# Batch 0's last pairs in another order, and w_in's loads cut at an eighth

## The chip, the core and the metric

The kernel runs on one core of a Trainium2 chip. The metric is the device time of one execution in microseconds (us). The core has five engines that run side by side and meet at semaphores: TensorE (PE, matmuls; its weight loads are shown apart as PEld), VectorE (DVE), ScalarE (ACT), GpSimd (POOL) and SyncE (SP). DMAs are issued by POOL's queue and by SP's queue and are carried by 16 shared DMA engines. A DMA that POOL issues also takes POOL some time to describe.

## The reference

Attention with a window of 32 tokens and 8 global tokens, for 8 batches, 8 heads, 576 tokens and 64 values a head; its output, 4608 tokens of 512, goes through two matrices with a snake function between them:

```python
scores = scale * np.matmul(q, k.transpose(0, 1, 3, 2))
mask = np.abs(pos[:, None] - pos[None, :]) <= window
mask = mask | is_global[:, None] | is_global[None, :]
scores = np.where(mask, scores, -1000000000.0)
...
attn = attn / (np.sum(attn, axis=-1, keepdims=True) + 1e-09)
x = np.matmul(attn, v)                    # then heads side by side: (4608, 512)
h = x @ w_in                              # (512, 2048)
s = np.sin(alpha * h)
g = h + s * s / (alpha + 1e-09)
out = g @ w_out                           # (2048, 512)
```

## The kernel before

**Stages.** The batches run one after the other: the attention of batch b+1 shares PE with gemm2 of batch b, and gemm1 of batch b+1 follows. The order of instructions on each engine is written out by hand; each engine takes its own in that order. Batch 0 has no gemm2 to run beside it: until about 28 us there is attention alone (`first_batch`), then gemm1(0), and at 51 us the attention of batch 1 with gemm2(0) begins.

**Attention.** Heads go in four pairs (`hp` 0 to 3, `last` is 3). For each pair `scores` makes products of queries and keys in PSUM, two parts with an Exp on ACT that writes the weights E, and `cover` multiplies E by the mask on DVE. `denominators(hp)` sums the weights with matmuls by ones into zd, then ACT takes a logarithm L (L772), SP stores it, and DVE sums eight columns for the global tokens (GD, L756). `inverse(hp)` is one Exp on ACT from L to R (L779; two buffers). `first_numerators(hp)` does `products(hp, 0)` (28 matmuls), `global_products` (8 matmuls) and `normalise`, which on DVE multiplies by R into xT (L908) and sums GN. In batch 0 the numerators of pairs 0 and 2 lie in the bank zr, those of pair 1 in zn, and those of pair 3, like all denominators, in zd. So each use of zd waits until L and GD have read the one before it.

**`set_recip`** turns alpha on PE (L710), copies it to alphaT (L711), adds 1e-9 (L712) and takes the reciprocal into recipT (L713), all on DVE behind the transpose. alphaT is the scale of gemm1's Sin (L1162); recipT enters gemm1's last step, H on DVE (L1168). `warm(z, n)` issues n spare matmuls of 128x512 into a bank that nobody reads (L569).

**gemm1** makes 16 groups of 128 columns (`nt`), each of 4 chunks (one for each pair of heads) in two halves. Groups 0 and 1 first do the chunks of pairs 0 to 2, six matmuls each, and then that of pair 3, which needs the last xT. Then come Sin on ACT, the square on ACT or DVE, and H on DVE.

**gemm2** multiplies H by w_out in blocks of 128 rows. gemm2(0) does, for its first two blocks, matmuls 0 to 7 of both ahead; then block 0 goes on with matmul 8. `fill(n)` issues the next n of them: 7 before the attention of batch 1 begins and 9 within its first pair, then 9 within the second.

**Loads.** POOL issues, in this order: lying copies of batch 0's q and k (`load_lying`), v (`load_v0`, 12 DMAs), the first part of w_in, then, after `pace` has waited for the last pair's weights E, the second part of w_in, batch 1's q and k for pairs 0 and 1, the third part of w_in, q and k for pairs 2 and 3, v of batch 1 (`cast_v(1)`, tile vd), and w_out in two halves (`load_w_out`, matmuls 0 to 7 and 8 to 15). They leave in order from one queue. Meanwhile SP's queue gathers the rows of the global tokens from v, k and q. `load_w_in(lo, hi)` counts in quarters of the 2048 columns, so its first part, `load_w_in(0, 1)`, covers groups 0 to 3, the second groups 4 to 7, the third 8 to 15.

Of the kernel before, what the change touches and what calls it, by code (L numbers as in the profile page):

```python
# [249 lines left out]
def kernel(  # L250
# [13 lines left out]
    DM, DFF = moe_w_in.shape  # L264
# [83 lines left out]
    def cast_v(b):  # L348
        cast_heads(b, v, "vd")

    def pace(src):

        nc.gpsimd.tensor_copy(out=seen[0 : src.shape[0]], in_=src)
# [43 lines left out]
    def edge_tile(half):  # L397
        r, o = half * D, (1 - half) * D
        m = (1 - half) * NT6
        nc.vector.tensor_copy(out=VX[0][r : r + KT, m], in_=VX[0][o : o + KT, 1 if m else NT6 - 1])  # L400
# [21 lines left out]

    def load_w_in(lo, hi):
        if lo < hi:
            cols = slice(lo * DFF // 4, hi * DFF // 4)
            nc.gpsimd.dma_start(
                out=w_in[:, :, cols], in_=moe_w_in[:, cols].rearrange("(c p) n -> p c n", p=P)
            )
# [24 lines left out]
    def load_lying(b, w, hps):  # L453

        hs = slice(2 * hps.start, 2 * hps.stop)
        nc.gpsimd.dma_start(
            out=lie[b][D * w : D * w + NU, hs],
            in_=(q, k)[w][b, hs].rearrange("h (u r) d -> u h (r d)", r=NR),
        )
# [3 lines left out]
    zo = [banks.tile([P, 512], DT.float32, name=f"zo{i}") for i in range(2)]  # L463
# [103 lines left out]
    def warm(z, n):  # L567
        for _ in range(n):
            nc.tensor.matmul(  # L569
                out=z[:], lhsT=ones[:], rhs=ones[:][:, None, :].to_broadcast([P, 4, P]),  # L570
                start=True, stop=True, skip_group_check=True,
            )
# [133 lines left out]
        nc.tensor.matmul(out=zo[0][:], lhsT=pick[:], rhs=VGb[:], start=True, stop=True, skip_group_check=True)  # L706
        nc.vector.tensor_copy(out=VGT[:].rearrange("p h d -> p (h d)"), in_=zo[0][:])

    def set_recip():
        nc.tensor.transpose(out=zo[0][:, 0:NT], in_=arow[:], identity=idf[0:NT, 0:NT])  # L710
        nc.vector.tensor_copy(out=alphaT[:], in_=zo[0][:, 0:NT])  # L711
        nc.vector.tensor_scalar(out=recipT[:], in0=alphaT[:], scalar1=1e-9, scalar2=None, op0=ALU.add)  # L712
        nc.vector.reciprocal(out=recipT[:], in_=recipT[:])  # L713

# [39 lines left out]
    def global_sums(b, hp, key, z):  # L754
        g0 = z[:, 0, 0, 0:4]
        nc.vector.tensor_reduce(  # L756
            out=(GN, GD)[key][:, hp, :, b].rearrange("p (c x) -> p x c", x=2),
            in_=bass.AP(
                tensor=g0.tensor, offset=g0.offset,
                ap=[list(g0.ap[0]), [256, 2], [1, 4], [512, 2], [SEG, 4]],  # L760
            ),
            axis=AX.XY, op=ALU.add,
        )

    def tokens(z):
        return z.rearrange("p k x c -> p (k x) c")[:, :, 0 : 3 * SEG].rearrange(
            "p k (m c) -> p k m c", c=SEG
        )[:, :, :, 4:]
# [8 lines left out]
    def inverted(L):  # L777
        R = normp.tile([P, 4, 3, KT], DT.float32, name="R")
        nc.scalar.activation(out=R[:], in_=L[:], func=AF.Exp, scale=-1.0, bias=shift[:, 0:1])  # L779
        return R  # L780

    def attention(b, beside):
# [43 lines left out]
        def weights(hp, g):  # L826
            return Es[hp][:, :, G3 * g : G3 * (g + 1), :].rearrange("p t m c -> p t (m c)")

        def cover(hp, g):
            Eg = weights(hp, g)  # L830
            nc.vector.tensor_tensor(  # L831
                out=Eg, in0=Eg,
                in1=MASKT[:, None, G3 * g : G3 * (g + 1), :].rearrange("p o m c -> p o (m c)").to_broadcast(
                    [P, 2, G3 * WCOL]
                ),
                op=ALU.mult,
            )

        def nd(hp, key):


            if b == 0:
                t = zd if key or hp == last else (pair["zr"], zn)[hp % 2]
            else:
                t = (zn, zd)[key] if hp < last else (pair["zr"] if key else zd)
            return t[:].rearrange("p k (x c) -> p k x c", x=2)

        def products(hp, key):


            for e in range(NT6 + 1):
                for half in range(2):
                    i, m, c0, c1 = windows(half)[e]
                    s0 = begin(i)
                    lo, hi = (0, CUT + 4) if half == 0 else (CUT, QLEN)
                    if e == NT6:
                        lo, hi = (lo, CUT) if half == 0 else (CUT + 4, hi)
                    a, z = max(s0 + c0, lo), min(s0 + c1, hi)
                    rows = slice(half * D, half * D + NK)
                    for t in range(2):  # L860
                        bank = (hp, key, half, t)
                        nc.tensor.matmul(  # L862
                            out=nd(hp, key)[t * D : (t + 1) * D, half, :, a - half * CUT : z - half * CUT],
                            lhsT=ones[rows, 0:D] if key else values(b, rows, half, i, 2 * hp + t),
                            rhs=Es[hp][rows, t, m, :].rearrange("p (x c) -> p x c", x=2)[:, :, a - s0 : z - s0],
                            start=bank not in begun, stop=True, skip_group_check=True,
                        )
                        begun.add(bank)

        def global_products(hp):  # L870


            for half in range(2):
                rows = slice(half * D, half * D + NK)
                for t in range(2):
                    for x in range(2):
                        e0 = Es[hp][rows, t, 0, 60 * x + 20 : 60 * x + 21]
                        nc.tensor.matmul(
                            out=nd(hp, 0)[t * D : (t + 1) * D, half, x, 0 : 3 * SEG].rearrange(
                                "p (m c) -> p m c", c=SEG  # L880
                            )[:, :, 4:],
                            lhsT=VGT[rows, 2 * hp + t, :],
                            rhs=bass.AP(
                                tensor=e0.tensor, offset=e0.offset,
                                ap=[list(e0.ap[0]), [2 * WCOL, 3], [WCOL - 4, 2], [1, 24]],
                            ),
                            start=False, stop=True, skip_group_check=True,
                        )
# [6 lines left out]
        def inverse(hp):  # L895
            Rs[hp] = inverted(Ls[hp])

        def first_numerators(hp):
            products(hp, 0)
            global_products(hp)  # L900
            normalise(hp)
# [5 lines left out]
        def normalise(hp):  # L907
            nc.vector.tensor_tensor(  # L908
                out=xT[:, hp, 0:S].rearrange("p (k m c) -> p k m c", k=4, c=KT), in0=tokens(nd(hp, 0)),
                in1=Rs[hp][:], op=ALU.mult,  # L910
            )
            global_sums(b, hp, 0, nd(hp, 0))
# [6 lines left out]
        def first_batch():  # L919

            for hp in range(NHP):
                Es[hp] = pairp.tile([P, 2, NT6, WCOL], DT.bfloat16, name="E")
                for g in range(2):
                    scores(hp, g)
                    if hp == 0:
                        cover(hp, g)
                if hp == last:
                    pace(Es[hp][0:1, 0, 0, 0:1])
                    load_w_in(1, 2)
                    for hps in (early, late):  # L930
                        for w in (1, 0):
                            load_lying(1, w, hps)
                        if hps == early:
                            load_w_in(2, 4)
                    for half in (1, 0):
                        edge_tile(half)
                    nc.gpsimd.tensor_copy(out=seen[0:1], in_=VX[0][0:1, NT6, 0, 0:1])
                    cast_v(1)
                    load_w_out((0, 1))
                beside(hp)  # L940
                for g in range(2 * (hp > 0)):
                    cover(hp, g)
                if hp:
                    denominators(hp - 1)
            release_ring()
            for hp in range(2):
                inverse(hp)
                first_numerators(hp)
            set_recip()
            inverse(last - 1)  # L950
            denominators(last)
            first_numerators(last - 1)
            warm(zo[1], 1)
            products(last, 0)
            global_products(last)
            inverse(last)
            nc.scalar.preload_act_table(AF.Sin)
            warm(zo[1], 2)
            normalise(last)
            pair["after"].release()  # L960

        last = NHP - 1
# [434 lines left out]
```

## Time and profile before

| | |
|---|---|
| median of three runs | 338.68 us (338.3 to 339.26) |
| the profiled execution's own time | 338.49 us |
| its span, first to last instruction | 336.8 us |
| PE busy | 316.2 us, 94% |
| ACT, DVE, POOL busy | 277.1, 255.9, 143.7 us |
| granted TensorE clock | 0.996 |
| HBM read and written | 41.95 MB, 20.77 MB |

The span is what the trace covers; the profiled execution's time holds in addition what lies around it. The times of single instructions below all come from this one execution, in microseconds from the start of the span. A row of the timeline gives start, length, engine, line, operation and tiles, and in brackets how long the engine stood idle before it and on whose account; "issue" means that the profile shows nothing that the engine waited for.

### The profile page before, as it was taken

The numbers are of one execution on the slowest core, as the hardware profiler recorded it, in microseconds if no ns is written. First come the engines' busy times: TensorE is split into PE (matmuls) and PEld (weight loads), VectorE is DVE, ScalarE is ACT, GpSimd is POOL, SyncE is SP. The second block draws the span as 40 slices with busy tenths as digits, with TensorE's granted clock in tenths as the row PEclk, the third lists the DMA queues.
The fourth block names the chain that finished last, engine by engine and source line by source line (L and its number), as shares of the span: only waits on it lengthen the run. The fifth ranks groups of instructions, "written<-read, shape, count | busy, mean of one in ns | idle before, by whom it ended". The sixth has DMA issues, their size and how long they took to land.

```text
span 336.8 us, 11878 instructions
## 1 busy us (share of the span) xinstructions
PE 316.2 (94%) x4812; PEld 202.8 (60%) x4812; DVE 255.9 (76%) x488; ACT 277.1 (82%) x402; POOL 143.7 (43%) x296
## 2 busy tenths in 40 slices
PE   0778999999999999999999999999999999999993
PEld 0765765577556765667556755676567745665553
DVE  4885896887887788688877788778868888788930
ACT  6775888989998889988998889889898898889611
POOL 7983324349516670666355652487060000004500
PEclk9999999999999999999999999999999999999998
DMA  7999999999989998999969993899999311010232
GB/s 104 114 162 205 186 226 169 152 166 135 181 143 133 190 124 137 94 119 186 151 93 137 172 162 85 131 176 136 132 111 133 65 60 42 1 33 8 73 93 69
DMA packets 141942, 42.01 MB, mean 125 GB/s; under 512 B 126426, under 2 KB 136794, under 8 KB 141882
## 3 DMA queue, kind: packets, MB, share of 16 engines
q0 software_dynamic: 100096, 18.51, 71.1%
q1 hardware_dynamic: 41786, 22.69, 34.1%
q8 instruction: 38, 0.62, 0.8%
q14 instruction: 22, 0.18, 0.2%
HBM read 41.95 MB, written 20.77 MB: 186 GB/s over the span
## 4 chain that ended last, share of the span: by engine, by line
PE 87%; DVE 4%; ACT 3%; issue 2%; DMA 1%; POOL 1%; DVEq 0%; POOLq 0%
PE zo L1220 38%; PE zn L1115 14%; PE zr L1115 11%; PE zd L1115 10%; PE ring L814 4%; PE zd L862 4%; PE zn L862 2%; DVE H L1168 2%; DMA g0k<-in_k_dram,grow 1%; ACT sb L1162 1%; PE zn L814 1%; PE zr L862 1%; DVE recipT L712 1%; DVE s L1167 1%; PE zo L630 1%
## 5 line engine op out<-in xcount | busy, mean ns | idle before, releaser
L1220 PE MATMUL zo<-w_out,H 128*128 128x512 bf16 (+1 forms) x576 | 147.1, 377 | 0.3 <-DVE KX L637 0.3
L1115 PEld LDWEIGHTS <-w_in 128*128 128x128 bf16 x1024 | 100.1, 98 | 43.9 <-issue 8.3
L1220 PEld LDWEIGHTS <-H 128*128 128x128 bf16 x592 | 53.7, 98 | 46.2 <-issue 0.4
L1115 PE MATMUL zn<-xT,w_in 128*128 128x288 bf16 (+1 forms) x384 | 57.7, 290 | 1.6 <-DVE H L1168 1.4
L1115 PE MATMUL zr<-xT,w_in 128*128 128x288 bf16 x320 | 48.0, 288 | 0.3
L1168 DVE SCALAR_TENSOR_TENSOR H<-s,recipT,zn 128x576 bf16<-128x576 bf16 (+1 forms) x48 | 39.4, 822 | 10.4 <-ACT s L1165 6.5
L1162 ACT ACTIVATE sb<-zn,alphaT 128x576 bf16<-128x576 f32 (+1 forms) x48 | 35.7, 743 | 13.7 <-PE zn L1115 13.2
L1115 PE MATMUL zd<-xT,w_in 128*128 128x288 bf16 x320 | 46.3, 288 | 0.3 <-DVE H L1168 0.2
L822 ACT ACTIVATE E<-ring 128x720 bf16<-128x720 f32 x46 | 35.9, 780 | 8.3 <-PE ring L814 7.7
L1167 DVE TENSOR_TENSOR s<-sb 128x576 bf16<-128x576 bf16 (+1 forms) x70 | 32.6, 465 | 12.2 <-ACT sb L1162 12.0
L1165 ACT ACTIVATE s<-sb 128x576 bf16<-128x576 bf16 (+1 forms) x58 | 40.0, 689 | 1.8
L831 DVE TENSOR_TENSOR E<-E,MASKT 128x720 bf16<-128x720 bf16 x64 | 33.5, 529 | 7.6 <-ACT E L822 5.6
L1168 DVE SCALAR_TENSOR_TENSOR H<-s,recipT,zd 128x576 bf16<-128x576 bf16 (+1 forms) x40 | 32.9, 822 | 7.6 <-ACT s L1165 5.0
L1168 DVE SCALAR_TENSOR_TENSOR H<-s,recipT,zr 128x576 bf16<-128x576 bf16 (+1 forms) x40 | 32.9, 822 | 6.6 <-ACT s L1165 5.0
L344 POOL DMA_DIRECT2D kd<-in_k_dram x48 | 31.4, 657 | 10.4 <-issue 8.0
L1162 ACT ACTIVATE sb<-zd,alphaT 128x576 bf16<-128x576 f32 (+1 forms) x40 | 29.6, 740 | 5.2 <-PE zd L1115 5.1
L1162 ACT ACTIVATE sb<-zr,alphaT 128x576 bf16<-128x576 f32 (+1 forms) x40 | 29.6, 740 | 4.3 <-PE zr L1115 4.3
L1210 POOL COPY H<-H 128x11 bf16 (+1 forms) x16 | 7.2, 453 | 57.6 <-DVE H L1168 56.7
L346 POOL DMA_DIRECT2D vd<-in_v_dram x48 | 30.5, 645 | 1.7 <-issue 1.3
L346 POOL DMA_DIRECT2D qd<-in_q_dram x40 | 25.4, 635 | 6.0 <-issue 6.0
L1227 ACT COPY osb<-zo 128x512 f32<-128x512 f32 (+1 forms) x33 | 19.1, 580 | 10.6 <-PE zo L1220 7.0
L814 PEld LDWEIGHTS <-KX 64*64 64x64 bf16 x896 | 15.8, 112 | 19.4 <-issue 19.0
(171 smaller groups left out, 377.7 us busy)
## 6 DMA issues: line engine op xcount, KB each, us to landing
VF<-vd SPq DMA_DIRECT2D x14, 336.0 KB
kd<-in_k_dram POOLq DMA_DIRECT2D x48, 72.0 KB, 4.8
vd<-in_v_dram POOLq DMA_DIRECT2D x48, 72.0 KB, 4.1
qd<-in_q_dram POOLq DMA_DIRECT2D x40, 72.0 KB, 5.5
w_out<-in_moe_w_out_dram POOLq DMA_DIRECT2D x2, 1024.0 KB, 25.7
out_dram<-osb SPq DMA_DIRECT2D x7, 256.0 KB
out_dram<-osb SPq DMA_DIRECT2D x8, 224.0 KB
out_dram<-osb SPq DMA_DIRECT2D x8, 192.0 KB
```

The lines of the kernel that those rows point to most:

```text
L344: nc.gpsimd.dma_start(out=dst[:, :, h], in_=src.rearrange("(i a) d -> a i d", a=KT))
L346: nc.gpsimd.dma_start(out=dst[:, h], in_=src)
L814: nc.tensor.matmul(out=z[half * D : (half + 1) * D, t, 0 : G3 * WCOL].rearrange("p (m x c) -> p m x c", x=2, c=60)[:, m % G3, :, c0:c1], l ...
L822: nc.scalar.activation(out=weights(hp, g), in_=z[:, :, 0 : G3 * WCOL], func=AF.Exp, scale=scale)
L831: nc.vector.tensor_tensor(out=Eg, in0=Eg, in1=MASKT[:, None, G3 * g : G3 * (g + 1), :].rearrange("p o m c -> p o (m c)").to_broadcast([P, ...
L862: nc.tensor.matmul(out=nd(hp, key)[t * D : (t + 1) * D, half, :, a - half * CUT : z - half * CUT], lhsT=ones[rows, 0:D] if key else values ...
L1115: nc.tensor.matmul(out=h_part, lhsT=w_in[:, c, nt * P : (nt + 1) * P], rhs=xT[:, c, lo:hi], start=(c == 0), stop=(c == CT - 1), skip_group ...
L1162: nc.scalar.activation(out=sb[:, 0:W], in_=h, func=AF.Sin, scale=alphaT[:, nt : nt + 1])
L1165: nc.scalar.activation(out=s2[:, 0:W], in_=sb[:, 0:W], func=AF.Square)
L1167: nc.vector.tensor_tensor(out=s2[:, 0:W], in0=sb[:, 0:W], in1=sb[:, 0:W], op=ALU.mult)
L1168: nc.vector.scalar_tensor_tensor(out=H2[:, nt, r0 : r0 + W], in0=s2[:, 0:W], scalar=recipT[:, nt : nt + 1], in1=h, op0=ALU.mult, op1=ALU.add,)
L1220: nc.tensor.matmul(out=ops[:, cols], lhsT=H2[:, nt, blk * P : (blk + 1) * P], rhs=w_out[:, nt, cols], start=(nt == 0), stop=(nt == NT - 1) ...
```

## The change

`load_w_in` counts in eighths. The first call stays `load_w_in(0, 1)`, and so takes groups 0 and 1 alone; the second, behind the wait for the last pair's weights, takes groups 2 to 7; the third is the same as before. Their number and their place among POOL's other issues stay.

In batch 0 pair 0's inverse moves ahead of pair 2's denominators. `set_recip` is split: the transpose and the copy to alphaT (`set_alpha`) come after pair 0's numerators, the add and the reciprocal after the last `normalise`. A spare matmul follows `set_alpha`. The last pair's denominators move ahead of the numerators of pairs 1 and 2, and pair 2's inverse behind these denominators.

```diff
     def load_w_in(lo, hi):
         if lo < hi:
-            cols = slice(lo * DFF // 4, hi * DFF // 4)
+            cols = slice(lo * DFF // 8, hi * DFF // 8)
...
-    def set_recip():
+    def set_alpha():
         nc.tensor.transpose(out=zo[0][:, 0:NT], in_=arow[:], identity=idf[0:NT, 0:NT])
         nc.vector.tensor_copy(out=alphaT[:], in_=zo[0][:, 0:NT])
+
+    def set_recip():
         nc.vector.tensor_scalar(out=recipT[:], in0=alphaT[:], scalar1=1e-9, scalar2=None, op0=ALU.add)
         nc.vector.reciprocal(out=recipT[:], in_=recipT[:])
...
                     pace(Es[hp][0:1, 0, 0, 0:1])
-                    load_w_in(1, 2)
+                    load_w_in(1, 4)
...
-                            load_w_in(2, 4)
+                            load_w_in(4, 8)
...
                     cover(hp, g)
+                if hp == last:
+                    inverse(0)
                 if hp:
                     denominators(hp - 1)
             release_ring()
-            for hp in range(2):
-                inverse(hp)
-                first_numerators(hp)
-            set_recip()
-            inverse(last - 1)
+            inverse(1)
+            first_numerators(0)
+            set_alpha()
+            warm(zo[1], 1)
             denominators(last)
-            first_numerators(last - 1)
+            inverse(2)
+            first_numerators(1)
+            first_numerators(2)
             warm(zo[1], 1)
             products(last, 0)
             global_products(last)
...
             warm(zo[1], 2)
             normalise(last)
+            set_recip()
```

## The prediction

> **What bounds the kernel now.** I read the page first (its own execution took 338.49 us for a span of 336.8 us; the median of the three runs is 338.68), then busy time by stage, the chain of waits from 20 to 36 us, each engine's timeline there, and last the DMA issues with their landings. By stage (columns: stretch, its length, then PE, PEld, DVE, ACT and POOL busy, clock, DMA share, GB/s):
>
> ```profile
> 20.20:31.50 11.30, 9.80 (x221) 7.16 (x221) 7.72 (x16) 5.91 (x9) 8.12 (x11) 1.00 1.19 201
> 31.50:51.30 19.80, 17.86 (x338) 13.11 (x336) 17.64 (x27) 17.82 (x28) 4.56 (x5) 1.00 1.44 206
> 51.30:56.20 4.90, 4.86 (x100) 2.52 (x100) 3.06 (x5) 3.72 (x6) 1.38 (x3) 1.00 1.81 180
> 56.20:75.00 18.80, 18.80 (x353) 11.57 (x342) 15.15 (x31) 17.55 (x27) 8.20 (x17) 1.00 1.31 157
> 75.00:330.00 255.00, 254.31 (x3440) 159.66 (x3439) 199.43 (x361) 216.87 (x314) 104.60 (x226) 1.00 1.02 114
> ```
>
> From 56.2 us on PE idles 0.7 of 273.8 us: whatever time PE has when it enters that stretch reaches the end of the kernel whole. The change lies in the first row, and in the transfers that run until 56. In the first row the chain of waits reads (start, length, what):
>
> ```profile
> 24.23 2.14 DVE recipT L712
> ...
> 26.78 0.79 PE zd L862 x25
> ...
> 28.80 1.44 PE zn L1115 x6
> 30.24 0.93 PE zr L1115 x6
> ...
> 31.46 0.75 ACT sb L1162
> ...
> 34.82 0.98 PE zr L1115 x8
> ```
>
> So the reciprocal's first half (the add on recipT) holds up the last pair's products into zd (26.78), the spare matmuls, gemm1's first groups, and the first Sin at 31.46. The second bound is not in this chain. It is the second half of w_out, the transfer that gemm2(0) needs for its row blocks' ninth matmul. POOL's issues, what their landings took, PE when that half is first used, and two slices of DMA rate:
>
> ```profile
> 16.50 0.87 POOL L426 DMA_DIRECT2D w_in<-in_moe_w_in_dram  x1
> 19.88 0.76 POOL L426 DMA_DIRECT2D w_in<-in_moe_w_in_dram  x1
> 23.79 2.16 POOL L334 DMA_DIRECT2D vd<-in_v_dram  x1
> 27.63 0.89 POOL L432 DMA_DIRECT2D w_out<-in_moe_w_out_dram  x1 [0.80 <-DMA w_in<-in_moe_w_in_dram]
> ```
> ```profile
> DMA to landing us min/median/max: 6.3/7.5/14.1
> ```
> ```profile
> w_out<-in_moe_w_out_dram POOLq DMA_DIRECT2D x1, 1024.0 KB, 28.6
> ```
> ```profile
> 56.23 2.10 PE L1220 MATMUL zo<-w_out,H 128*128 128x512 bf16 x9
> ```
> ```profile
> 18.00:19.00 1.00, 0.51 (x14) 0.40 (x14) 0.82 (x3) 0.93 (x3) 0.86 (x1) 1.00 1.06 62
> 20.00:21.00 1.00, 1.00 (x37) 0.76 (x40) 0.65 (x1) 0.60 (x1) 1.00 (x2) 1.00 1.23 200
> ```
>
> The middle row is w_in's three loads: 16.50 + 6.3 = 22.8, 19.88 + 7.5 = 27.4. The second half of w_out lands at 27.63 + 28.6 = 56.2, and PE starts on it at 56.23. That is the 17th matmul of gemm2(0): 7 at the start and 9 in the first pair use the first half only, and the next 9 go to block 0's ninth. PE takes them in order. So there is no slack between that landing and PE: whatever the change gains before 56.2, PE gives back there unless the landing comes earlier too.
>
> **The change part by part: the reordered tail of batch 0.** PE's rows (start, length, what, idle before), and how many matmuls lie between two of its idle times:
>
> ```profile
> 19.26 0.51 PE L814 MATMUL zn<-QX,KX 64*64 64x120 bf16 x14 [0.51 <-issue]
> ...
> 20.24 0.79 PE L862 MATMUL zd<-E,ones 56*64 56x88 bf16 x28
> 20.86 0.77 PE L862 MATMUL zr<-E,VF 56*64 56x88 bf16 x28
> ...
> 21.68 0.78 PE L862 MATMUL zn<-E,VF 56*64 56x88 bf16 x28
> ...
> 22.66 0.28 PE L710 MATMUL zo<-idf,arow 16*128 16x16 f32 x1
> 22.87 0.49 PE L862 MATMUL zd<-E,ones 56*64 56x88 bf16 x12
> 24.38 0.51 PE L862 MATMUL zd<-E,ones 56*64 56x120 bf16 x16 [1.02 <-issue]
> 24.67 0.82 PE L862 MATMUL zr<-E,VF 56*64 56x88 bf16 x28
> ...
> 25.69 0.61 PE L569 MATMUL zo<-ones 128*128 128x512 bf16 x1
> 26.78 0.79 PE L862 MATMUL zd<-E,VF 56*64 56x88 bf16 x28 [0.48 <-DVE GD L756]
> ...
> 27.77 1.03 PE L569 MATMUL zo<-ones 128*128 128x512 bf16 x2
> 28.60 1.65 PE L1115 MATMUL zn<-xT,w_in 128*128 128x288 bf16 x6
> ```
> ```profile
> 15.20:19.24 4.04, 2.79 (x128) 1.00 1.30 96
> 19.24:24.36 5.12, 4.10 (x128) 1.00 1.18 188
> ```
> ```profile
> 21.09 0.65 ACT L772 ACTIVATE L<-zd 128x576 f32<-128x576 f32 x1 [0.48 <-PE zd L862]
> ...
> 24.94 0.65 ACT L772 ACTIVATE L<-zd 128x576 f32<-128x576 f32 x1 [0.94 <-PE zd L862]
> ```
> ```profile
> 21.96 0.22 DVE L756 TENSOR_REDUCE GD<-zd 128x8 f32<-128x64 f32 x1
> ...
> 26.40 0.25 DVE L713 RECIPROCAL recipT<-recipT 128x16 f32<-128x16 f32 x1
> 26.57 0.16 DVE L756 TENSOR_REDUCE GD<-zd 128x8 f32<-128x64 f32 x1
> ...
> 32.81 0.81 DVE L1168 SCALAR_TENSOR_TENSOR H<-s,recipT,zn 128x576 bf16<-128x576 bf16 x1
> ```
>
> In the new order PE keeps everything to 20.86, then pair 0's numerators (36 matmuls, 20.86 to 21.68 = 0.82), the transpose 0.98 after their start (as 21.68 to 22.66) at 21.84, the added spare matmul 0.21 later (as 22.66 to 22.87) at 22.05 for 0.5 (two take 1.03 at 27.77), so the last pair's denominators start at 22.55. They need zd read by GD (21.96 + 0.22): met. L follows 0.85 after that start (20.24 to 21.09 in the pair before): 23.4 instead of 24.94, if PE runs through. The inverse moved ahead of the logarithm delays that earlier logarithm by at most 0.2 us, and GD at 21.96 waits for the masks anyway. The new GD comes right after L, at 24.1 instead of 26.57, because the 2.14 + 0.25 us of reciprocal are no longer ahead of it. Behind the denominators: pair 1's numerators at 23.17 (0.62 after, as 20.24 to 20.86), pair 2's at 24.0, the spare matmul at 25.0 (1.02 after, as 24.67 to 25.69), the last products at 25.5. Against 26.78 that is some 1.2 us earlier. The last inverse needs the buffer of pair 1's R, free at about 25.1, ahead of the last xT: nothing.
>
> The stall of 1.02 us at 24.38 does not vanish, it moves. It comes 128 matmuls, each with its weight load, after the one at 19.26, as that came 128 after the one at 15.23, whatever the code does there. In the new order the 128 run out after 14 + 1 + 28 + 36 + 1 + 1 + 28 = 109 and 19 of pair 1's numerators, at about 23.6. If what PE waits for still comes at 24.38, then 9 products and 8 more (0.42) bring pair 2 to 24.8, the last products to 26.4: a gain of 0.4 instead of 1.2. The Trainium skill, Runtime: NRT & Kernel Launch, section Instruction fetch mechanics, says that an engine's instructions come in blocks of 256 that it fetches by DMA while it runs; by that rule the stall is tied to the block, and the gain is 0.4. The trace agrees with the spacing of 256; no run yet shows the stall elsewhere.
>
> Then the chunk matmuls. The first six run at 0.24 us each (1.44), the next six in 0.93, later groups at 0.12 (8 in 0.98). If the change of pace stays at its hour, a start 1.2 earlier saves only about 0.6 at the first Sin; if it moves along, 1.2; if the fast pace held from the first chunk on, 12 x 0.12 = 1.47 instead of 2.37, 0.9 more: 2.1. The Trainium skill, TensorE: Matmul & The Clock Gate, section The two states you'll see, says that full clock comes after about 3.4 us of sustained work; by it the denser PE of the new order could have it that early, and the gain would be 2.1, an estimate. The granted clock reads 1.00 in both stretches, so the slow pace shows in the rows' lengths alone. By the rows g, the lead with which gemm1 begins, is 0.4 to 2.1; I take 1.2. It holds through 51.3 (ACT 17.82 and DVE 17.64 of 19.80 busy), and ends at 56.2.
>
> set_recip after the last xT: the add took 2.14 beside POOL's descriptor writing (23.79 for 2.16) where the reciprocal of the same tile took 0.25. In its new place it costs 0.25 to 2.14, done by about 30; its first reader is H at 32.81 less g, and only that group's s is queued behind it. Zero. If the cover went, up to 2.1.
>
> **w_in.** Same bytes and same three issues, so POOL's time is the same. Groups 0 and 1 come with the first load; groups 2 and 3 move into the second, which by the sum of bytes lands where it did, at 27.4, perhaps 1 later; group 2 is used two groups after 28.6 - g, from about 29.4: hidden by 1 to 2 us. POOL's second half of w_out waits for that landing before its issue at 27.63; 1 later it is still 20 us ahead of its turn. What the change can cost is a hole in POOL's queue: the second load's issue stays at 19.88 (paced on the weights), and the queue needs about 1.6 to 2 us from issue to traffic (16.50 to the 62 GB/s of 18 to 19). So the second load flows from about 21.6, while an eighth, half of the old 18.5 to 22.8, is through at 20.5 to 21.2. The hole is 0.4 to 1.1 us. Everything behind it in that queue moves by it: lying q and k, vd, both halves of w_out. Some comes back, because the gathers on SP's queue and the fetch of instructions use the hole, and a landing waits for the last of the 16 DMA engines, which may still be on the first load while the others run dry. Bounds for the landing at 56.2: -0.2 (the fastest run is 0.2 below this execution) to +1.1; I take +0.2, nearer the lower end, since only the last engine counts.
>
> **The sum.** Gain g of 1.2 before 56.2, lost to the landing; the landing +0.2; 338.49 + 0.2 = 338.7 us, level with the median of 338.68.
>
> **Rivals.** First, the gate isn't there in timed runs (the landing comes 1 us or more before PE, as the other transfers do): then g arrives whole, 338.49 - 1.2 = 337.3, or, at the fast pace from the first chunk, 336.4. For it: the change does cut the chain; zero slack in one execution can be a coincidence. Against it: 28.6 us in a queue that is 200 GB/s all along. Second, slower: the hole in POOL's queue passes to w_out undiminished, +1.1, and PE stands at the ninth matmul until 57.3: 339.6; it decides from a shift of 1.0 on. For it: the 62 GB/s after a late issue. Against it: the gathers fill it. Third, the change does not do what it says: the block stall falls into pair 1's numerators, g is 0.4 or less, 338.1 to 338.5, which is no change either.
>
> **How the numbers follow.** About 0.3% (1.0 us) is what a measurement of this kernel tells from no change. Forecast (gate at w_out, landing within -0.2 to +0.9): 0.45. Small gain from the stall: 0.17, also within. No gate: 0.25, nearly all of it faster by over 1.0. Hole: 0.13, nearly all slower. So 0.24 faster, 0.63 same, 0.13 slower. The likeliest case's own range is 338.2 to 339.4; that of 8 in 10 goes to the first rival's 337.2 and the second's 339.7.
>
> **What would show it.** Right: recipT's add behind the last xT; no idle of PE ahead of the last products on GD; L of the last pair near 23.5; the first Sin at 29.4 (g of 2.1) to 31.1 (g of 0.4); and at the ninth matmul of block 0 an idle PE that waits for the DMA of w_out, to 56 to 57. Wrong: w_out's second half landing well before PE gets there, or the block's stall over 1 us in pair 1's numerators.

## The result and the profile after

| | before | after |
|---|---|---|
| median of nine runs each, side by side | 338.7 us (338.11 to 340.08) | 341.36 us (339.55 to 342.87) |
| ratio after/before, 95% interval | | 1.0068 [1.0045, 1.0092] |
| profiled execution, its span | 338.49 us, 336.8 us | 342.25 us, 340.6 us |
| granted TensorE clock over the span | 0.996 | 0.991 |

The changed kernel is slower by 0.7%, 2.3 us by the ratio. That lies outside the predicted range. The profiled execution is one of the slower of the nine: its span is 3.8 us longer, so one part of what follows is particular to it. Its trace has 3380 matmul records from 75 us on where before has 3440, at almost the same count of weight loads (3432 and 3439), so PE's lower busy time there is records that are missing and no saving. Busy time by stage of the kernel after, in the columns of the first fence of the prediction:

```profile
20.20:31.50 11.30, 10.27 (x224) 7.30 (x216) 7.19 (x19) 7.57 (x11) 7.85 (x11) 1.00 1.08 176
31.50:51.30 19.80, 18.14 (x342) 12.75 (x344) 18.06 (x28) 17.37 (x26) 4.55 (x5) 1.00 1.43 205
51.30:56.20 4.90, 3.22 (x93) 1.92 (x91) 2.13 (x4) 3.53 (x6) 2.48 (x5) 1.00 1.51 196
56.20:75.00 18.80, 16.99 (x314) 9.82 (x319) 12.33 (x26) 13.75 (x22) 4.35 (x9) 0.91 1.21 138
75.00:330.00 255.00, 247.63 (x3380) 159.17 (x3432) 201.53 (x363) 218.53 (x316) 107.09 (x231) 1.00 1.03 116
```

PE is denser in the first row (10.27 of 11.30 busy, 9.80 before) and idles in the third, where before it idled 0.04 us. The fourth row has a clock of 0.91. The next two fences show why. First two steps of the chain of waits of the kernel after (start, length, what), then PE's timeline (start, length, what, idle before it and on whose account):

```profile
27.53 29.85 DMA w_out<-in_moe_w_out_dram
57.38 0.04 issue
```
```profile
22.15 0.79 PE L864 MATMUL zd<-E,ones 56*64 56x88 bf16 x28
...
49.58 1.68 PE L1226 MATMUL zo<-w_out,H 128*128 128x512 bf16 x6 [0.91 <-DMA w_out<-in_moe_w_out_dram]
...
54.05 0.47 PE L864 MATMUL zd<-E,ones 56*64 56x88 bf16 x28
57.43 3.56 PE L1226 MATMUL zo<-w_out,H 128*128 128x512 bf16 x8 [2.90 <-DMA w_out<-in_moe_w_out_dram]
...
100.08 0.41 PE L864 MATMUL zd<-E,ones 56*64 56x120 bf16 x20 [0.81 <-issue]
```

At block 0's ninth matmul PE stands 2.90 us and waits for w_out's second half, which lands at 27.53 + 29.85 = 57.38 instead of 56.2. The wait is long because PE is early as well as the transfer late. Then come the matmuls themselves: 3.56 us for the run that took 2.10 before. The windows of the kernel after say what happened there (columns as above; the last but two is the granted clock):

```profile
57.90:61.30 3.40, 3.40 (x25) 1.20 (x28) 0.72 (x1) 0.59 (x1) 0.00 (x0) 0.50 2.12 137
```

PE ran at half the clock for 3.4 us. The sum by PE's and ACT's marks: it enters the ninth matmul at 57.43 instead of 56.23 (+1.20) and leaves that run at 60.99 instead of 58.33 (+2.66). At batch 1's first Sin, where before has

```profile
69.50 0.74 ACT L1162 ACTIVATE sb<-zn,alphaT 128x576 bf16<-128x576 f32 x1
```

the kernel after has

```profile
72.37 0.74 ACT L1168 ACTIVATE sb<-zn,alphaT 128x576 bf16<-128x576 f32 x1
```

which is +2.87. The stall of 0.81 at 100.08 brings that to the 3.8 of the spans (2.87 + 0.81 = 3.7, 0.1 unassigned). Two of the twelve kernels below have it before the same matmul (0.92 in after with less in the queue, 1.10 with an early quarter of w_in), the kernel before does not. Over the nine runs the granted clock splits in the same manner: the five at 0.991 to 0.993 took 341.35 to 342.87 us, the three at 0.997 and 0.998 took 339.55 to 340.49, and one at 0.995 took 341.36. Half the clock for 3.4 us is 1.7 us, 0.005 of 340, so a run that contains such a stretch can read 0.995 at most. The clock is at half behind PE's last matmul as well (2.5 us in before, which therefore reads 0.996), so a low reading alone does not prove a stretch in the middle.

Why the transfer is late stands in three slices of DMA rate (last column, GB/s), before:

```profile
21.00:22.00 1.00, 1.00 (x56) 1.00 (x52) 0.97 (x4) 0.92 (x2) 1.00 (x3) 1.00 1.26 205
22.00:23.00 1.00, 1.00 (x41) 0.76 (x37) 0.75 (x3) 1.00 (x2) 1.00 (x2) 1.00 1.12 172
```

after:

```profile
20.00:21.00 1.00, 1.00 (x56) 1.00 (x52) 0.97 (x2) 1.00 (x3) 1.00 (x3) 1.00 0.75 121
21.00:22.00 1.00, 1.00 (x23) 0.48 (x14) 1.00 (x4) 0.97 (x2) 1.00 (x2) 1.00 0.97 46
22.00:23.00 1.00, 1.00 (x41) 0.85 (x44) 0.63 (x3) 0.00 (x1) 1.00 (x3) 1.00 0.83 127
```

and in POOL's issues of the kernel after:

```profile
16.75 0.81 POOL L426 DMA_DIRECT2D w_in<-in_moe_w_in_dram  x1
19.63 0.76 POOL L426 DMA_DIRECT2D w_in<-in_moe_w_in_dram  x1
```

The second w_in load is still issued at 19.63, and the eighth that was issued at 16.75 is through before that load flows. From 20 to 23 us before moved 200 + 205 + 172 = 577 KB, after 121 + 46 + 127 = 294 KB. The missing 283 KB are 1.4 us at 200 GB/s. From 18 to 20 us after had moved 60 KB more (105 + 155 against 62 + 138), which leaves 223 KB, 1.1 us; the landing at the end of that queue came 1.2 us later.

### The profile page after: what moved, and what is told of

Same layout as the page of the kernel before. It is cut to its first block, busy times and chain, and to the rows that moved or that the text cites. A ratio compares the mean times of both kernels' runs of the same rounds, so it can differ in the third digit from the quotient of the medians.

```text
span 340.6 us, 11822 instructions
## 1 busy us (share of the span) xinstructions
PE 311.2 (91%) x4754; PEld 202.8 (60%) x4813; DVE 254.9 (75%) x488; ACT 277.1 (81%) x402; POOL 143.1 (42%) x296
## 4 chain that ended last, share of the span: by engine, by line
PE 78%; DMA 10%; POOL 4%; issue 3%; ACT 2%; DVE 2%; POOLq 0%; DVEq 0%
PE zo L1226 34%; PE zn L1121 13%; PE zd L1121 9%; PE zr L1121 9%; DMA w_out<-in_moe_w_out_dram 9%; PE ring L816 4%; PE zd L864 3%; PE zn L864 2%; DMA H<-in_q_dram 1%; DVE H L1174 1%; POOL H L456 1%; ACT sb L1168 1%; PE zr L864 1%; POOL vd L334 1%; PE zd L1270 1%
## 5 line engine op out<-in xcount | busy, mean ns | idle before, releaser
L1226 PE MATMUL zo<-w_out,H 128*128 128x512 bf16 (+1 forms) x517 | 135.7, 379 | 9.6 <-issue 5.1
L1121 PE MATMUL zn<-xT,w_in 128*128 128x288 bf16 (+1 forms) x384 | 57.0, 287 | 2.2 <-DVE H L1174 1.4
L1168 ACT ACTIVATE sb<-zd,alphaT 128x576 bf16<-128x576 f32 (+1 forms) x40 | 29.6, 740 | 5.1 <-PE zd L1121 5.1
L1168 ACT ACTIVATE sb<-zr,alphaT 128x576 bf16<-128x576 f32 (+1 forms) x40 | 29.6, 740 | 4.3 <-PE zr L1121 4.3
```

Of the source, the lines that this page charges most:

```text
L1121: nc.tensor.matmul(out=h_part, lhsT=w_in[:, c, nt * P : (nt + 1) * P], rhs=xT[:, c, lo:hi], start=(c == 0), stop=(c == CT - 1), skip_group ...
L1168: nc.scalar.activation(out=sb[:, 0:W], in_=h, func=AF.Sin, scale=alphaT[:, nt : nt + 1])
L1226: nc.tensor.matmul(out=ops[:, cols], lhsT=H2[:, nt, blk * P : (blk + 1) * P], rhs=w_out[:, nt, cols], start=(nt == 0), stop=(nt == NT - 1) ...
```

## The experiments

The account under test, theory A of the expectations: w_in's split moves w_out's landing, PE comes early and stands at the ninth matmul, and the slow pace behind that wait adds the rest. The rivals are that the new order itself costs the time, that the second load of w_in does so elsewhere, and that the wait is there but costs nothing. Kernels of one group ran on one chip against the kernel before (medians 339.09, 339.68 and 339.3 us in the three groups), twelve runs each. Three profiled executions (w_in's split alone, the spare matmuls, and after with less in the queue) are the slowest of their twelve, so their rows show a mechanism, and the cost is read from the ratio.

**One part alone.** The new order with w_in in quarters as before:

```diff
-            cols = slice(lo * DFF // 8, hi * DFF // 8)
+            cols = slice(lo * DFF // 4, hi * DFF // 4)
...
-                    load_w_in(1, 4)
+                    load_w_in(1, 2)
...
-                            load_w_in(4, 8)
+                            load_w_in(2, 4)
```

> Batch 0's new order, w_in's loads in quarters as before. Theory A (w_out's second half is the gate; the split of w_in alone moves its landing, by +1.2 us after the change): the landing comes back to about 56.2, PE reaches block 0's ninth matmul 1 to 2.4 us early and stands there; time 338.7, up to 1.4 more if PE is slow after the wait as it was after the change (9 matmuls in 3.56 instead of 2.10). Theory B (the new order itself costs, by whatever way): 341, landing unimportant. Theory C (w_in's split costs, but not through w_out): 336.5, the lead arrives whole.

Measured 339.46 us, ratio 1.0007 [0.9989, 1.0024]: the order alone costs nothing and gains nothing. PE's timeline of this kernel:

```profile
23.26 0.66 PE L864 MATMUL zn<-E,VF 56*64 56x88 bf16 x19
24.44 0.35 PE L864 MATMUL zn<-E,VF 56*64 56x120 bf16 x9 [0.52 <-issue]
...
56.52 2.10 PE L1226 MATMUL zo<-w_out,H 128*128 128x512 bf16 x8 [0.59 <-DMA w_out<-in_moe_w_out_dram]
```

The stall has moved to exactly the twentieth of pair 1's numerators (19 before it), and w_out's wait is 0.59, to 56.52; no slow pace follows it.

The split of w_in alone, in the order of before, is the reverse of that diff applied to the kernel before.

> w_in's loads cut at an eighth, batch 0's order as before. A: w_out's second half lands at about 57.4 and PE, which comes at 56.2, waits 1.2 there; 339.9, without the slow pace. B: 338.7, no change. C: 341 with the loss elsewhere than at block 0's ninth matmul.

Measured 339.92 us, ratio 1.0029 [1.0011, 1.0047]: slower by itself, and by less than the whole change (the two intervals only touch, at 1.0045 to 1.0047). Its timeline and one window:

```profile
57.23 0.59 PE L1220 MATMUL zo<-w_out,H 128*128 128x512 bf16 x1 [2.63 <-DMA w_out<-in_moe_w_out_dram]
```
```profile
56.90:60.30 3.40, 2.85 (x7) 1.14 (x8) 1.58 (x2) 0.01 (x1) 0.57 (x1) 0.50 2.42 156
```

In this execution, the slowest of its twelve, the wait and the 3.4 us at half clock are there without the new order. PE came early here too: at 54.13 to the denominators that stand at 55.80 in before and at 54.05 in after. So the wait is 2.63, and not the 1.2 that was expected of a PE that comes at 56.2. Eight of the twelve runs read a clock of 0.997 or more and cannot contain such a stretch; three of after's nine do. So most of the 0.29%, 1.0 us, is paid without the slow pace, and it is the size of the landing's shift here (27.59 + 29.6 = 57.2 instead of 56.2).

**The gate taken away.** In gemm2(0)'s first two blocks the second half of w_out is not used, the first half's rows being multiplied twice (so that part of the output is another sum). Done in the kernel after and in the one before:

```diff
-                    ... rhs=w_out[:, nt, cols],
+                    ... rhs=w_out[:, nt % 8 if b == 0 and blk < lo + 2 else nt, cols],
```

> The whole change, but gemm2(0)'s first two row blocks use the first half of w_out in place of the second (those two blocks are computed from wrong weights); all loads stay. A: no wait at the ninth matmul, the lead of 2.2 us arrives whole: 336.3 to 336.7. B and C: 340 to 341, since the loss lies elsewhere.

> The kernel before with the same replacement of w_out's second half in gemm2(0)'s first two row blocks (computed from wrong weights). A: PE came to the ninth matmul just as the half landed, so 338.0 to 338.7, as before or a little under where other executions waited. B and C: 338.7. Against the third kernel, A expects 2 us between them, B that this one is the faster.

Measured 339.3 us, ratio 0.9999 [0.9978, 1.0019], for after, and 338.95 us, 0.9999 [0.9979, 1.0019], for before. The gate costs before nothing, and the whole loss of after hangs on it: 1.0068 falls to 0.9999. But PE's lead does not reach the end: the 336.3 to 336.7 us that A expected were missed by over 2.5. PE comes to batch 1's first denominators at 54.05 in after without the gate and at 55.51 in before without it, 1.46 ahead. The timeline of after without the gate, from its wait for w_out's first half on, shows where that stays:

```profile
49.58 1.69 PE L1226 MATMUL zo<-w_out,H 128*128 128x512 bf16 x6 [1.95 <-DMA w_out<-in_moe_w_out_dram]
...
54.69 1.89 PE L1226 MATMUL zo<-w_out,H 128*128 128x512 bf16 x8 [0.16 <-issue]
...
57.21 0.49 PE L864 MATMUL zn<-E,VF 56*64 56x88 bf16 x26 [0.31 <-DMA VF<-VGb]
...
60.76 0.21 PE L864 MATMUL zd<-E,ones 56*64 56x32 bf16 x3 [1.28 <-issue]
```

0.31 goes to batch 1's values and 1.28 to a stall of the kind that falls each 128 matmuls: 1.59, the whole lead. (A row of 0.16 on "issue" in front of gemm2's matmuls is a missing record.) At batch 1's first Sin the two kernels are level, after without the gate first, then before without it:

```profile
69.82 0.74 ACT L1168 ACTIVATE sb<-zn,alphaT 128x576 bf16<-128x576 f32 x1
```
```profile
69.61 0.74 ACT L1162 ACTIVATE sb<-zn,alphaT 128x576 bf16<-128x576 f32 x1
```

The kernel before goes through the same denominators without a stall, and reaches the last of them at about the hour at which after resumes:

```profile
60.23 0.49 PE L862 MATMUL zd<-E,ones 56*64 56x88 bf16 x28
```

**The hole closed.** The second w_in load right behind the first, no longer paced on the weights:

```diff
     load_w_in(0, 1)
+    load_w_in(1, 4)
...
                     pace(Es[hp][0:1, 0, 0, 0:1])
-                    load_w_in(1, 4)
```

> The whole change, but w_in's second load (groups 2 to 7) is issued right behind the first, without the wait for the last pair's weights. A: no hole in POOL's queue, w_out's second half back at 56.2 or up to 0.5 earlier; but the fetch of instructions has to pass the same traffic as before, so a stall of 0.5 to 1 us is back in pair 1's numerators and the lead is 0.3 to 1; 338.7 to 339.4, as the new order alone (339.46). If the hole is not the cause of the late landing, the landing stays at 57.4 and the time at 340.5 to 341.4.

Measured 339.97 us, ratio 0.9998 [0.9975, 1.0021]. One slice of it, with the columns as before, and PE's timeline:

```profile
21.00:22.00 1.00, 1.00 (x56) 0.97 (x48) 0.97 (x3) 1.00 (x2) 1.00 (x2) 1.00 1.14 194
```
```profile
26.64 0.35 PE L865 MATMUL zn<-E,VF 56*64 56x120 bf16 x9 [2.44 <-issue]
...
57.46 2.11 PE L1226 MATMUL zo<-w_out,H 128*128 128x512 bf16 x9
```

No hole (194 GB/s where after had 46) and no wait at the ninth matmul. The landing is back where it was:

```profile
28.41 0.88 POOL L432 DMA_DIRECT2D w_out<-in_moe_w_out_dram  x1 [1.97 <-DMA w_in<-in_moe_w_in_dram]
```
```profile
DMA to landing us min/median/max: 23.9/25.8/27.6
```

28.41 + 27.6 = 56.0, against 57.4 in after, 57.2 with the split alone and 57.3 (27.79 + 29.5) in after without the gate; with w_in in quarters it is 56.2 in before and 56.5 (27.30 + 29.2) with the new order alone. So the hole is what makes the landing late. PE comes to the ninth matmul later here, at 57.46, since the 128-matmul stall now takes 2.44 in the head; the loss is gone all the same, and nothing is won. Landing and lead changed together in this kernel, so it does not part their shares.

**The slow pace alone.** Eleven spare matmuls into an idle bank of batch 1's ring, ahead of the ninth matmul, fill PE's wait (the diff leaves out that `warm` is made to take such a bank):

```diff
...
+            if (b, hp) == (1, 1):
+                warm(zs[:, 0], 11)
             fill((SECOND_FIRST if b == 1 else SECOND)[hp])
```

> The whole change, with 11 spare matmuls of 128x512 on PE between batch 1's first denominators and block 0's ninth matmul (2.4 us at 0.22 each, in the place of most of the wait of 2.9). If the slow pace behind the wait (9 matmuls in 3.56 us, not 2.1) comes of PE having stood idle, it goes, and the time is 1.4 us under the change's: 340. If it comes of something else (contention with the transfers), it stays: 341.4. In no theory is it faster than before.

Measured 340.49 us, ratio 1.0031 [1.0007, 1.0055]. In the profiled execution the clock stays up:

```profile
56.89 2.53 PE L569 MATMUL ring<-ones 128*128 128x512 bf16 x11 [0.40 <-ACT E L824]
```
```profile
57.90:61.30 3.40, 3.40 (x17) 1.37 (x15) 1.76 (x3) 1.03 (x3) 1.46 (x3) 1.00 2.40 156
```

Ten of its twelve runs have a granted clock above the 0.995 of a run with such a stretch; three of after's nine have. The loss goes from 0.68% to 0.31%. That is 0.37% or 1.25 us for the slow pace, by ratios of different groups whose intervals overlap: the clock is shown, its price is only of the right size. In the profiled execution the half lands at 30.64 + 28.0 = 58.6 and the spare matmuls run to 59.26, so they hold PE up a little themselves. What remains, about 1 us, is the size of the landing's shift, and of the loss with w_in's split alone.

**Less in the queue ahead of w_out.** Two attempts. In the first, batch 1's late lying loads are left out and the early pairs' rows used for the late pairs too (so batch 1's late pairs hold other values), in after and in before:

```diff
...
-                        for w in (1, 0):
+                        for w in (1, 0) if hps == early else ():
```

> The whole change with two of POOL's loads left out: batch 1's lying q and k for pairs 2 and 3, 576 KB as written, ahead of vd and w_out in the queue (those two pairs are computed from pairs 0 and 1). Theory A, widened after the first four runs (not one landing but the whole stream of loads up to 60 us, with both halves of w_out, batch 1's values and the fetches of instructions in it, bounds batch 1's start): everything behind comes about 3 us earlier, w_out at 46.5 and 54.3, and of the lead of 2.4 to 3.9 us some 2 arrive: 336.5 to 337. Theory D (the lead is lost to something else behind 50 us, such as PE's pace): 339 to 341.

> The kernel before with the same two loads left out (pairs 2 and 3 of batch 1 from pairs 0 and 1). A: the kernel before is bound by its engines up to 56 us and only touches the stream, so 338.5 to 339, as before or half a us less; then the change in this pair of kernels is worth 2 us of gain. D: 339, and no difference to the fifth kernel but the one that the change has anyway.

Measured 339.08 us, 0.9984 [0.9957, 1.0011], and 340.87 us, 1.0044 [1.0017, 1.0072]. These two don't answer the question, because the edit makes a wait of its own, in both kernels: the late pairs' transposes now read rows at a place that gemm1's groups of H overwrite, and wait for that write. PE's timeline of before with it:

```profile
49.40 0.73 PE L630 MATMUL zo<-identb,H 48*64 48x48 bf16 x39 [1.49 <-DVE H L1168]
```

What they do show is that a wait of this size, with little work around it and not for w_out, is followed by the slow pace as well (after with the edit, where PE stood 1.49 us to 47.49):

```profile
47.30:50.70 3.40, 3.21 (x50) 2.26 (x51) 1.62 (x3) 1.04 (x2) 0.00 (x0) 0.50 1.21 215
```

In the second attempt batch 0's last four groups use the weights of the four before them (so H is other numbers there), and the last quarter of w_in follows behind batch 2's q:

```diff
...
-                            load_w_in(4, 8)
+                            load_w_in(4, 6)
...
                 cast_heads(2, q, "qd")
+                load_w_in(6, 8)
```

> The whole change, but w_in's columns for groups 12 to 15 are loaded behind batch 2's q, after 60 us, and not ahead of vd and w_out (in batch 0 those four groups use the weights of groups 8 to 11): 512 KB less as written, some 2.6 us at 200 KB a us. The two loads left out of e5 and e6 had made gemm1's H wait for lying rows that it overwrites, 2.9 us in both; here nothing new is waited for. Theory A (the stream of loads up to 60 us bounds batch 1's start): w_out lands at about 47 and 54.8, PE hardly waits, the lead of 2.4 to 3.9 arrives at 2 or so, 336.8 to 337.5 where before is 339. D (lead lost behind 50 us whatever the stream): 339 or more.

> The kernel before with the same columns loaded after 60 us (batch 0's groups 12 to 15 use the weights of groups 8 to 11). A: as before within half a us, 338.6 to 339.2, since PE comes no earlier than in the kernel before; 1.5 to 2.2 us over the ninth kernel. D: as before, and no difference to the ninth kernel in its favour.

Measured 340.33 us, 1.0025 [1.0001, 1.0049], and 340.01 us, 1.0014 [0.999, 1.0038]. In after PE gets the second half at 54.55 instead of 57.43, and loses the lead right behind it:

```profile
54.55 2.10 PE L1227 MATMUL zo<-w_out,H 128*128 128x512 bf16 x8 [0.55 <-DMA w_out<-in_moe_w_out_dram]
...
59.79 0.21 PE L864 MATMUL zd<-E,ones 56*64 56x32 bf16 x3 [0.77 <-issue]
...
67.66 0.21 PE L864 MATMUL zn<-E,VF 56*64 56x32 bf16 x4 [2.06 <-issue]
```

Two stalls of 0.77 and 2.06, and this execution then has half clock for 3.4 us from 67.9 on. Its runs spread from 338.78 to 342.65, so no more than the loss becoming smaller is to be read from it.

**Other ways to keep the lead.** A first quarter of w_in ahead of v's loads, so that the queue has more in hand:

```diff
+    load_w_in(0, 2)
     load_v0()
-    load_w_in(0, 1)
+    load_w_in(2, 3)
...
-                    load_w_in(1, 4)
+                    load_w_in(3, 4)
```

> The whole change with w_in's loads in another order: the first quarter ahead of v's twelve DMAs (between 11 and 17 us the transfers run at about half the rate of later, because POOL describes v's small pieces one after the other), the third eighth behind them, the fourth behind the wait for the last pair's weights. All is loaded and computed. A: the stream behind is about 2 us earlier than before, w_out's second half at 54 to 55, the lead of 2.4 arrives in good part: 337 to 337.8, faster than both kernels. Against it: POOL's one issue more (0.8) and w_in's traffic beside the early fetches of instructions; if these cost batch 0 over 2 us, 339 or more.

Measured 340.52 us, 1.0042 [1.0022, 1.0062]. No wait at w_out, but the head is later, with the longest of all the block stalls:

```profile
17.72 0.38 PE L865 MATMUL zd<-E,ones 56*64 56x120 bf16 x9 [3.37 <-issue]
```

Last, the new order with w_in in quarters and w_out's second half in two loads of four row blocks, gemm2(0) doing twelve matmuls of both blocks before it needs the last four:

```diff
...
-                    load_w_out((0, 1))
+                    load_w_out(((0, 8), (8 // 4, 4), (12 // 4, 4)))
...
-        ahead = {0: NT // 2, B - 1: SOON}.get(b, 0)
-        for blk in (lo, lo + 1):
-            yield from products(blk, bank(blk), range(ahead), full)
+        ahead = {0: 3 * NT // 4, B - 1: SOON}.get(b, 0)
+        for part in ((range(8), range(8, 12)) if b == 0 else (range(ahead),)):
+            for blk in (lo, lo + 1):
+                yield from products(blk, bank(blk), part, full)
```

> The new order alone, w_in in quarters as before, and w_out's second half in two DMAs, matmuls 8 to 11 and 12 to 15, with block 1's 8 to 11 ahead of block 0's 12: the last part is needed 8 matmuls and a pair's attention later, about 58. A: the small lead of 0.3 arrives and no execution waits at 56: 338.4 to 338.9 where before is 339. If w_out is not what executions wait for, as before.

Measured 338.92 us, 0.9998 [0.998, 1.0016]: as fast as before and no faster. PE passes the gate without a wait, 1.6 us ahead of before's 56.23, and the same stall is behind it:

```profile
54.65 1.90 PE L1226 MATMUL zo<-w_out,H 128*128 128x512 bf16 x7
...
60.59 0.21 PE L864 MATMUL zd<-E,ones 56*64 56x32 bf16 x3 [1.28 <-issue]
```

That the lead past w_out is eaten by these stalls is read from the rows of three kernels; no kernel takes them away, so it is argued and not shown. That PE goes on at 60.76 and 60.59, when before gets to the same matmuls, suggests that it meets something there that comes at its own hour. None of the twelve is measurably faster than before.

## Why the prediction was wrong

**The gate: right.** The step that PE and w_out's second half meet with no slack held, and so did the sign that it gave for it: PE idle at the ninth matmul until 56 to 57 (57.43). With the gate taken away, after stands level with before.

**The landing: mis-sized.** The step by which the hole costs 0.4 to 1.1, some of it comes back and the landing moves by +0.2 is the first that failed: the landing moved by 1.2, which is the whole hole (1.1 to 1.4 by the missing bytes) and a little above its upper bound. The gathers on SP's queue did not fill it: 46 GB/s in the slice where they were to. The second rival had the mechanism, the place and a price of +1.1; it got 0.13. With the hole closed, the half lands at 56.0 and the loss is gone.

**The slow pace: missing.** No term of the sum and no rival priced what a wait does to the work behind it. The sum took a wait of PE as idle time alone; 2.9 us of it were followed by 3.4 us at half clock, worth 2.66 - 1.20 = 1.46 us at the end of the run of matmuls. With it the second rival's 339.6 would have read 341.1, against a median of 341.36. The prediction used the clock gate only for the start of gemm1, though from 31.50 us on every stage of before is at full clock, so that an idle stretch made by the change could only lose it. (The 1.00 of its first row is no reading: the trace of before has no clock record before 30.5 us, and the rows' lengths show half the pace there, as the prediction saw.) The Trainium skill, TensorE: Matmul & The Clock Gate, section The two states you'll see, has PE fall to half clock after an idle window of about 3.4 us and take such a window to come back. The return agrees with the 3.40 us at 0.50; the fall came after 2.90 here, after 2.06 in after with less in the queue, and after 1.49 and some short matmuls in the light-loads kernels, so less than a whole window of standing still is enough. Not each wait does it: the wait of 0.59 with the new order alone did not, nor did the 1.95 for w_out's first half in after without the gate. So the length of the wait alone does not decide. In these traces a stretch at full clock that ends in half clock is a whole multiple of 3.413 us long (30.72 in after, 20.48 in the light-loads kernels, 40.96 in after with less in the queue); that it matters where in this grid a wait falls is likely, and no run varies it.

**The gain of the new order: credited to the wrong part.** The lead came in larger than taken. ACT and DVE of after:

```profile
23.00 0.65 ACT L774 ACTIVATE L<-zd 128x576 f32<-128x576 f32 x1 [1.03 <-PE zd L864]
...
29.04 0.74 ACT L1168 ACTIVATE sb<-zn,alphaT 128x576 bf16<-128x576 f32 x1 [2.15 <-PE zn L1121]
```
```profile
27.25 0.17 DVE L714 TENSOR_SCALAR recipT<-alphaT 128x16 f32<-128x16 f32 x1
```

L came at 23.00 (23.4 predicted), the denominators at 22.15 (22.55), and the first Sin at 29.04, a lead of 2.42 where the bound was 2.1. But the order makes the smaller part of it. The first Sin with the new order alone, then with w_in's split alone in the old order:

```profile
31.13 0.74 ACT L1168 ACTIVATE sb<-zn,alphaT 128x576 bf16<-128x576 f32 x1 [3.11 <-PE zn L1121]
```
```profile
28.30 0.74 ACT L1162 ACTIVATE sb<-zn,alphaT 128x576 bf16<-128x576 f32 x1 [1.91 <-PE zn L1115]
```

Against before's 31.46 that is a lead of 0.33 for the order (1.7 in its other trace, the one with w_out in three loads) and of 3.16 for the split (before's other traces, with edits that lie later, have it at 30.51 to 32.52). The prediction took the split for a cost alone. In the traces its hole goes with a head in which the block's stall is missing, and PE reaches the full pace sooner: with the split alone the first six chunk matmuls take 0.90 from 26.39, in before 1.65 from 28.60. So in these executions the split both brings PE early to w_out and makes w_out late; of the two the prediction had the second only.

The add of recipT, 2.14 in before's execution, takes 0.17 in its new place. It also takes 0.17 in the old one, in before without the gate:

```profile
23.74 0.17 DVE L712 TENSOR_SCALAR recipT<-alphaT 128x16 f32<-128x16 f32 x1
```

Of the five traces in the old order two have it long, before and before with less in the queue:

```profile
25.08 2.11 DVE L712 TENSOR_SCALAR recipT<-alphaT 128x16 f32<-128x16 f32 x1
```

The others have 0.71 (fewer lying loads) and 0.17 twice. POOL describes vd's load beside the short ones too (from 23.57 for 2.16 in before without the gate), so that alone does not make it long. That the reciprocal holds up the last pair's products is true of some executions only, and the term for its removal was no fixed property of the kernel.

The lead shrinks to 1.75 at PE's 54.05 (before came to that row 0.43 ahead of 56.23, at 55.80), as the wait of 0.91 for w_out's first half at 49.58 takes its part.

**The stall of each 128 matmuls.** The third rival's mechanism is right, and the new order alone shows it to the matmul: 19 numerators, then the stall. In after it is missing from the head, where the DMA queues had their hole, and is back with 2.44 where the hole is closed. The same holds over all the traces: the six with the split as in after (the split alone, the gate taken away, fewer lying loads, the spare matmuls, less in the queue, and after itself) have no stall at that block, and of the eight others seven have one of 0.24 to 2.44. The rule that the prediction cites from the Trainium skill, Runtime: NRT & Kernel Launch, section Instruction fetch mechanics, blocks of 256 instructions fetched by DMA, fits all of that; that the hole let the block come sooner is an inference from these kernels. The Trainium skill's word there that the cost of crossing a block is mostly hidden agrees with before from 56.20 us on (3793 matmuls, some 29 blocks, with 0.7 us idle in all); it does not hold for the head, where a crossing cost up to 3.37 us, nor for the kernels that came early past w_out.

**The range.** Its upper end of 339.7 was the second rival's price with no pace in it. A wait of PE that is forecast as a rival belongs in the range with all that follows from it, and 341.1 would have been that end; of the 0.9 by which the profiled execution lies above the median, 0.81 would be the stall at 100.08, which no step of the prediction had.

## What to carry to other kernels

A wait put in front of a dense engine costs its length and then what that engine loses in pace: price both, and look for rows where the clock is full only because nothing has ever stopped. Run each part of a change alone before it is credited with a gain: here the part that was taken for a cost brought most of the lead. When a load is made smaller but the issue of the next one stays tied to an event, count the bytes in hand until that next one flows; whatever lies behind it in the queue moves by the whole gap, up to the transfer that has no slack. Take no term from a single long instance of an instruction (2.14 us) when the one beside it of the same size takes 0.25.

## What the runs showed of the hardware

PE's clock read 0.50 for 3.4 us after waits of 2.90 and 2.63 us at w_out, after a stall of 2.06, and after a wait of 1.49 among short matmuls; a wait of 1.95 elsewhere left it at 1.00, and so did eleven spare matmuls in the place of the wait at w_out. A load cut to an eighth, with the next one still issued at 19.63, left DMA slices of 121, 46 and 127 GB/s where there were 200, 205 and 172, and a transfer some 35 us further down the queue landed 1.2 us later. A lead gained in the head, 1.5 to 1.7 us at w_out, did not once come out at the end: in the three kernels that had it there, stalls of the kind that falls each 128 matmuls (1.28 in two, 0.77 and 2.06 in the third) stand within the next 13 us.
